# First batch entry's attention products in two sets of PSUM banks, the first inner blocks in accumulator banks, the first pair's scores head by head, and decoding order 1.5 places ahead

## The chip, the cores and the metric

One core of a Trainium2 chip runs the whole program. The metric is the device time in microseconds; times are medians over several executions. A measurement of this kernel tells 0.2% from no change.

## The reference

Windowed attention (8 batch entries, 8 heads, 576 positions, head size 64) and then a gated MLP over all 4608 tokens:

```python
def _attn_ref(q, k, v):
    window, dilation = 32, 4
    scores = scale * np.matmul(q, k.transpose(0, 1, 3, 2))
    rel = pos[:, None] - pos[None, :]
    mask_plain = (rel >= 0) & (rel < window)
    mask_dil = (rel >= 0) & (rel < window * dilation) & (rel % dilation == 0)
    ...  # first four heads plain, last four dilated
    scores = np.where(masks[None, :, :, :], scores, -1000000000.0)
    ...  # softmax over the keys
    return np.matmul(attn, v)

def _moe_ref(x, w_in, w_out):          # x: 4608 x 512, w_in: 512 x 2048, w_out: 2048 x 512
    h = x @ w_in
    g = h * (1.0 / (1.0 + np.exp(-1.702 * h)))
    return g @ w_out
```

q, k and v are float32, the two weights float64.

## The kernel before

**Work in order.** Heads go in pairs, so a batch entry has four pairs (k = 0 to 3 for the first). For each pair the scores are made (`scores`), the softmax runs on VectorE, ScalarE and GpSimd (`softmax`), the probabilities are transposed by VectorE (`ct`), and the product with v (`first_product` for the first entry) leaves the attention output in PSUM. It is drained as a high part (`xh`, by ScalarE) and a low part (`xl`, the remainder, by VectorE) in the tile `xs`; the last 64 positions go into `rests_x` and are stored for later. Then groups of 512 tokens run through the MLP. The first group, `main[0]`, starts as soon as the first entry's output is there; its inner blocks `up(f)` make 128 of the 2048 inner channels by twelve products of 128x512 (`hp_m`: three for each of four chunks of the model dimension), a gate (tanh on ScalarE, a multiply on VectorE), another split into `gh` and `gl`, and twelve products of the second matrix into four accumulator banks (`acc_m`). Attention of later entries runs between those products. After three such groups the rest runs in blocks of a seven-product scheme (`up_p`, `second_p` and so on), which the change does not touch.

**Decoding.** A weight arrives as float64 and is turned into two fp32r parts by `decode(n)`: two ScalarE steps, a sign step on ScalarE or VectorE, a shift on VectorE, an add on VectorE or GpSimd, a copy and a subtract. `order` says which weight comes as the n-th; each is 512 KB.

**PSUM.** There are eight banks: two under the tag `sp` (scores), one each under `hp` and `av`, and four which are first one tile `first_x` (pool `four`) and later the accumulators `acc0` to `acc3` (pool `quarters`, in the same place). All four products of the first entry write to `first_x`, each to one half of the columns of all four banks; the plan holds the four banks as one thing (`FOUR`), so a product waits until the one before it is drained. `hp_m_0` lies in `hp`, `hp_m_1` in `sp`, `hp_m_2` in `av`.

**What sets the order.** Every step is entered in a `Plan` with a cost per engine, an urgency, and the names that it reads and writes. The planner places all steps in time by these costs and writes the instructions of each engine in that order; in three further rounds (`ROUNDS`) it uses due times from the round before for all that lies behind `SINCE`. A step with a choice of engines goes where it ends first. While the plan shows PE idle in the first 60 us, it puts idle products in: small ones (32x16) early on, and 512-column products of `ident`, both into a tile in the bank `av`, by the function `warm`. An engine takes its instructions strictly in the written order. DMAs are issued on SP's queue (`load`).

Names that the prediction uses: L309 to L342 are the constants and masks; `plain` is the mask, brought into PSUM by a product with `ident` ahead of the scores; L490 the scores, L510 the maximum, L514 the exponential, L576 the first entry's products, L695 the transposes, L346, L348 and L353 the helpers `copy` and `pair`, L402, L403, L396 and L406 steps of `decode`, L863 the inner products, L872 the gate's multiply, L1258 and L1262 the idle products.

## Time and profile before

| | |
|---|---|
| median of three runs | 823.12 us (821.65 to 823.53) |
| profiled execution | 822.45 us, span 820.7 us |
| PE busy | 809.3 us, 99% of the span |
| VectorE, ScalarE, GpSimd busy | 669.0, 518.0, 328.4 us |
| chain that ended last | PE 97% |
| first inner product (L863) | at 25.62 us |
| mean granted clock of PE | 0.997 |

The span is cut by the profile into rows of instructions with a start, a duration and, in brackets, how long the engine stood idle before them and who ended that. "PE" is the matmul itself and "PEld" the weight load that stands with each; "issue" is time in which an engine waited for nothing that the profile shows.

### The profile page before, as it was taken

The page shows a single profiled execution, that of the slowest core. Times are in us where ns is not written, and L with a number is a line of the kernel's source. Part 1 is how long each engine was busy: PE and PEld are TensorE (multiplying, and loading weights), DVE is VectorE, ACT ScalarE, POOL GpSimd, SP SyncE. Part 2 cuts the span into 40 slices and gives each one's busy share as a digit, 9 for nine tenths or more (in the row PEclk, how much of TensorE's full clock was granted, in tenths as well). Part 3 has the DMA queues.
Part 4 walks back from the last instruction along what each step waited for, and adds up shares of the span by engine and source line. Part 5 has one row for each costly group of instructions (what it writes and reads, how often), then busy time and mean ns, then how long its engine had stood idle before and what let it go on. Part 6 is the DMA issues. An engine that isn't in the chain of part 4 may idle for free.

```text
span 820.7 us, 18890 instructions
## 1 busy us (share of the span) xinstructions
PE 809.3 (99%) x7279; PEld 653.4 (80%) x7279; DVE 669.0 (82%) x1081; ACT 518.0 (63%) x988; POOL 328.4 (40%) x294
## 2 busy tenths in 40 slices
PE   7999999999999999999999999999999999999997
PEld 4677878888887888778888888888888888888886
DVE  6898988888888876899889899996679885867575
ACT  7898986767577766786866654545456534544340
POOL 3442325455556553244345445531215332112251
PEclk9999999999999999999999999999999999999999
DMA  9577658899758657797788777775565658674545
GB/s 354 186 249 212 175 161 296 287 318 303 241 176 271 223 180 243 252 307 234 235 236 264 253 254 249 234 256 183 179 207 189 198 189 275 201 226 157 180 153 181
DMA packets 109610, 188.13 MB, mean 229 GB/s; under 512 B 26448, under 2 KB 55376, under 8 KB 109520
## 3 DMA queue, kind: packets, MB, share of 16 engines
q1 hardware_dynamic: 109376, 186.78, 70.2%
q8 instruction: 58, 0.95, 0.5%
q14 instruction: 32, 0.26, 0.1%
q10 hardware_dynamic: 144, 0.13, 0.0%
HBM read 140.64 MB, written 45.09 MB: 226 GB/s over the span
## 4 chain that ended last, share of the span: by engine, by line
PE 97%; DMA 1%; DVE 1%; issue 0%; ACT 0%; SPq 0%; DVEq 0%
PE hp_m L863 16%; PE up_p L1006 10%; PE up_r L1006 9%; PE up_q L1006 9%; PE acc_m L800 5%; PE second_p_Q L1121 5%; PE second_q_Q L1121 5%; PE acc_m L804 5%; PE acc_m L801 5%; PE second_r_Q L1121 5%; PE sp L490 4%; PE second_q_Z L1121 3%; PE second_r_Z L1121 3%; PE second_R L1121 3%; PE second_p_Z L1121 3%; PE av L608 2%
## 5 line engine op out<-in xcount | busy, mean ns | idle before, releaser
L353 POOL TENSOR_TENSOR arena<-arena 128x256 f32<-128x256 f32 (+3 forms) x94 | 100.7, 1083 | 97.8 <-DVE wi_last_units L353 21.6
L863 PE MATMUL hp_m<-xs,wi_kept 128*128 128x512 f32 x504 | 127.7, 396 | 1.2 <-DVE arena L872 0.9
L863 PEld LDWEIGHTS hp_m<-xs,wi_kept 128*128 128x128 f32 x504 | 92.9, 188 | 22.8 <-DVE arena L872 1.9
L353 POOL TENSOR_TENSOR wo_kept<-arena,wo_kept 128x512 fp32r<-128x512 f32 x41 | 56.9, 1395 | 131.5 <-ACT wo_kept L346 84.9
L346 ACT ACTIVATE wo_kept<-arena 128x512 fp32r<-128x512 f32 x111 | 69.2, 630 | 40.7 <-PE second_r_Q L1121 10.9
L1006 PE MATMUL up_r<-wi_kept,xs 128*128 128x512 f32 x336 | 85.3, 389 | 0.0
L1006 PE MATMUL up_p<-wi_kept,xs 128*128 128x512 f32 x336 | 84.2, 394 | 0.2 <-DVE arena L353 0.2
L1006 PE MATMUL up_q<-wi_kept,xs 128*128 128x512 f32 x336 | 83.4, 389 | 0.0
L1006 PEld LDWEIGHTS up_p<-wi_kept,xs 128*128 128x128 f32 x336 | 62.1, 188 | 14.7 <-DVE arena L353 0.9
L1006 PEld LDWEIGHTS up_q<-wi_kept,xs 128*128 128x128 f32 x336 | 63.0, 188 | 13.3 <-DVE arena L1028 0.3
L1006 PEld LDWEIGHTS up_r<-wi_kept,xs 128*128 128x128 f32 x336 | 63.1, 188 | 13.1
L353 DVE TENSOR_TENSOR wo_kept<-arena,wo_kept 128x512 fp32r<-128x512 f32 x80 | 61.1, 775 | 5.1 <-ACT wo_kept L346 4.7
L346 ACT ACTIVATE bt<-ct 32x256 f32<-32x256 f32 (+1 forms) x130 | 56.6, 435 | 11.7 <-DVE ct L534 6.0
L353 POOL TENSOR_TENSOR pr<-pr,sm 128x320 f32<-128x320 f32 x52 | 43.7, 856 | 48.5 <-DVE sm L518 43.5
L800 PE MATMUL acc_m<-gh,wo_kept 128*128 128x512 f32 x156 | 61.5, 394 | 0.0
L353 POOL TENSOR_TENSOR wo_kept<-wi_last_units,wo_kept 128x512 fp32r<-128x512 f32 x22 | 29.9, 1361 | 78.3 <-ACT wo_kept L346 72.3
L353 DVE TENSOR_TENSOR arena<-arena 128x512 f32<-128x512 f32 (+1 forms) x75 | 59.1, 797 | 2.7 <-ACT arena L346 1.8
L801 PE MATMUL acc_m<-gh,wo_kept 128*128 128x512 f32 x156 | 60.8, 390 | 0.0
L1027 ACT ACTIVATE arena<-arena 128x512 f32<-128x512 f32 x60 | 37.4, 628 | 33.4 <-DVE arena L353 27.2
L1028 DVE SCALAR_TENSOR_TENSOR arena<-arena 128x512 f32<-128x512 f32 x60 | 49.8, 837 | 1.7 <-ACT arena L1027 1.3
L346 ACT ACTIVATE gh<-arena 128x512 fp32r<-128x512 f32 x57 | 36.0, 631 | 17.5 <-DVE arena L872 5.8
L353 DVE TENSOR_TENSOR gl<-arena,gh 128x512 fp32r<-128x512 f32 x53 | 41.3, 779 | 6.5 <-ACT gh L346 3.2
(267 smaller groups left out, 1824.7 us busy)
## 6 DMA issues: line engine op xcount, KB each, us to landing
xs<-sums SPq DMA_DIRECT2D x168, 256.0 KB, 3.3
out_weights<-sums_o SPq DMA_DIRECT2D x63, 512.0 KB, 3.5
qk<-qk_dram SPq DMA_DIRECT2D x29, 576.0 KB, 4.4
xs<-sums_o SPq DMA_DIRECT2D x21, 512.0 KB, 3.8
v<-vp_dram SPq DMA_DIRECT2D x28, 320.0 KB, 4.1
sums_o<-arena SPq DMA_DIRECT2D x32, 256.0 KB, 3.2
sums<-arena SPq DMA_DIRECT2D x32, 256.0 KB, 2.9
arena<-wi_dram SPq DMA_DIRECT2D x15, 512.0 KB, 4.7
```

The lines of the kernel that those rows point to most:

```text
L346: A.activation(dst, src, AF.Copy, scale=scale)
L353: (V if e == DVE else G).tensor_tensor(out=dst, in0=a, in1=b, op=op)
L490: T.matmul(dst[:, w:w + n], u["qk"][rows, at:at + 32], u["qk"][rows, S + first:S + first + n], start=not masked(k), stop=True, tile_positi ...
L608: T.matmul(u["x"][i][rows, at:at + last - first], u["v"][keys, a, m], bt[keys, m, a, first:last], start=(bank_, a) not in begun, stop=True ...
L800: T.matmul(self.acc[j], w[:, 0, cols], high, start=f == 0, stop=False)
L801: T.matmul(self.acc[j], w[:, 1, cols], high, start=False, stop=False)
L804: T.matmul(self.acc[j], w[:, 0, P * j:P * j + P], low, start=False, stop=f == NF - 1)
L863: T.matmul(hps[f], wi(f)[:, st, cols], mv[:, c], start=c == 0 and k == 0, stop=c == NC - 1 and k == 2)
L1006: T.matmul(self.banks[place], xs[:, slot, at:at + P], wi_kept[:, 2 * a + c, mv], start=fresh and c == 0 and k == 0, stop=c == 1 and k == 2 ...
L1027: add({ACT: 0.60}, -10.0, lambda e: A.activation(unit(tmp), src(), AF.Tanh, scale=0.851), need, own(tmp))
L1028: add({DVE: -0.70 if need[0][0] == "A" else 0.70}, -10.0, lambda e: V.scalar_tensor_tensor(out=unit(dst), in0=unit(tmp), scalar=1.0, in1=s ...
L1121: T.matmul(self.second[key], w[:, st, cols], mv, start=fresh and y == 0 and k == 0, stop=y == 1 and k == 2, skip_group_check=True)
```

## The change

- The first entry's products alternate between two sets of four banks: pairs 0 and 2 in `first_x`, pairs 1 and 3 in the two banks of `sp` and in `hp` and `av`. Each pair of a set has its own columns. A product then no longer waits for the drain of the product before it, and the drains of pairs 1 and 3 come in three pieces, one for each tile.
- The first two inner blocks of the first group go to the accumulators `acc2` and `acc3`, since `sp`, `hp` and `av` are held by pairs 1 and 3; the third stays in `av`.
- Pair 0's q and k come in two transfers, one for each head, and its scores are two steps, one for each head.
- The decoding order is sorted by f for the first matrix and f + 1.5 for the second: wi0, wi1, wo0, wi2, wo1, wi3, wo2, wi4, where it was wi0, wi1, wo0, wi2, wo1, wo2, wi3, wo3.
- Pair 0's v is loaded later (urgency -4.5 instead of -6.7), `SINCE` is 140 instead of 130, and `warm` now gives no idle products from the moment at which pair 1's banks are taken.

```diff
-ROUNDS, SINCE, CALM, ROOM = 3, 130.0, 8.0, 3.0
+ROUNDS, SINCE, CALM, ROOM = 3, 140.0, 8.0, 3.0
-    order = [(0, 0), (0, 1), (1, 0), (0, 2)]
-    order += [(i % 2, i // 2) for i in range(2 * NF) if (i % 2, i // 2) not in order]
+    order = sorted(((out_, f) for f in range(NF) for out_ in range(2)), key=lambda b: b[1] + 1.5 * b[0])
...
-    FOUR = tuple(f"acc{j}" for j in range(NC))
+    SETS = tuple(f"acc{j}" for j in range(NC)), ("sp", "hp", "av")
...
+        if k == 0:
+            for a in range(2):
+                add({DMA: 295}, -9.0, lambda e, a=a: work(e, slice(D * a, D * a + D)), (), (("qk0", "head1")[a],))
+            return
...
-        u["x"] = first_x[:, :, ROW * (k % 2):ROW * (k % 2) + ROW]
+        cols = slice(ROW * (k // 2), ROW * (k // 2) + ROW)
+        if k % 2:
+            if "others" not in misc:
+                misc["others"] = bank([P, 2, GT], "sp", "first_sp"), *(bank([P, GT], n, f"first_{n}") for n in ("hp", "av"))
+            sp, hp, av = misc["others"]
+            u["x"] = [sp[:, :, cols], hp[:, None, cols], av[:, None, cols]]
+            parts = [sp[:, 0, cols], sp[:, 1, cols], hp[:, cols], av[:, cols]]
+        else:
+            u["x"] = [first_x[:, :, cols]]
+            parts = [first_x[:, g, cols] for g in range(4)]
...
-        add({PE: 1.5 if k else 2.3}, k - 1.0e5, lambda e: scores(k), (lots(k)[0],), ("sp", f"scores{k}"), count=180)
+        if k == 0:
+            for a in range(2):
+                add({PE: 0.75}, k - 1.0e5, lambda e, a=a: scores(k, (a,)), (("qk0", "head1")[a],), ("sp", f"scores{k}"), count=90)
+        else:
+            add({PE: 1.5}, k - 1.0e5, lambda e: scores(k), (lots(k)[0],), ("sp", f"scores{k}"), count=180)
...
-            FOUR, count=184)
+            SETS[k % 2], count=184)
...
-            place = {1: "sp", 2: "av"}.get(f, "hp") if self is main[0] else "hp"
+            place = {0: "acc2", 1: "acc3", 2: "av"}.get(f, "hp") if self is main[0] else "hp"
...
     def warm(i):
-        if 2 not in main[0].hps:
+        if "others" not in misc:
```

The written order shows the change on PE at two places. First the head of PE's program, before (idle products into `idle`, then the masks and scores of pair 0, `sp`; a number in a name only tells tiles apart):

```order
L1262 MATMUL idle<-ones 32x16 x49
L478 LDWEIGHTS ident
L478 MATMUL sp_189<-plain,ident 128x320
L478 LDWEIGHTS ident
L478 MATMUL sp_189<-plain,ident 128x320
L490 MATMUL sp_189<-qk_128 32x64 x35
```

The same place in the changed kernel, where L485 is the mask and L497 the scores:

```order
L1291 MATMUL idle<-ones 32x16 x44
L485 LDWEIGHTS ident
L485 MATMUL sp_183<-plain,ident 128x320
L497 MATMUL sp_183<-qk_128 32x64 x19
L497 MATMUL sp_183<-qk_128 32x48
L497 MATMUL sp_183<-qk_128 32x16
L485 LDWEIGHTS ident
L485 MATMUL sp_183<-plain,ident 128x320
```

There are five small idle products fewer, and the second head's mask has moved behind the first head's scores.

Second, PE before from pair 2's product on (`ct` is the transposed probabilities, v of pairs 1 to 3 lies in `arena`, `hp_m_0` and `hp_m_1` are the first two inner blocks); idle products stand between these rows and the products around them:

```order
L576 MATMUL first_x<-ct_91,arena 64x64 x24
L576 MATMUL first_x<-ct_91,arena 64x48 x8
L576 MATMUL first_x<-ct_91,arena 64x16 x8
L863 MATMUL hp_m_0_578<-xs,wi_kept 128x512 x3
L863 MATMUL hp_m_1_585<-xs,wi_kept 128x512 x3
```

In the changed kernel pair 3's product ends, and the inner blocks follow, as here:

```order
L592 MATMUL first_sp<-ct_92,arena 64x16 x4
L592 MATMUL first_hp<-ct_92,arena 64x16 x2
L592 MATMUL first_av<-ct_92,arena 64x16 x2
L892 MATMUL hp_m_0_668<-xs,wi_kept 128x512 x12
L892 MATMUL hp_m_1_695<-xs,wi_kept 128x512 x12
L892 MATMUL hp_m_2_718<-xs,wi_kept 128x512 x6
```

The inner products no longer come by threes between the attention products: all four of these stand first, with no idle products between them, and then whole inner blocks. (Idle products stand between the four sets of scores in both; those numbers are 2, 6 and 10 before, and 4, 10 and 11 now.)

Third, ScalarE in the changed kernel from pair 1's drain to pair 2's (`xs` are the high parts, `arena<-first_av` pair 1's rest, the L395 row is the 16-bit sign step of a decode):

```order
L346 ACTIVATE xs<-first_sp 128x288
L346 ACTIVATE xs<-first_hp 128x144
L346 ACTIVATE xs<-first_av 128x80
L346 ACTIVATE arena<-first_av 128x64
L346 ACTIVATE wo_kept<-arena 128x512
L395 ACTIVATE arena<-arena 128x512
L346 ACTIVATE xs<-first_x 128x4x128
```

Pair 1's high part has come apart into three pieces, and pair 2's stands behind a weight split and a sign step. On VectorE pair 2's low part stands as follows:

```order
L724 STREAM_TRANSPOSE ct_92<-pr_84 128x320 x2
L348 COPY arena<-first_x 128x4x16
L353 ISA arena<-bt,arena 128x1024
L353 TENSOR_TENSOR xs<-first_x,xs 128x4x128
```

Behind pair 3's transposes come pair 2's rest, one decode step, and then pair 2's low part.

## The prediction

> **What bounds the kernel now.** I read the page first: its busy line, and the chain that ended last.

> ```profile
> span 820.7 us, 18890 instructions
> PE 809.3 (99%) x7279; PEld 653.4 (80%) x7279; DVE 669.0 (82%) x1081; ACT 518.0 (63%) x988; POOL 328.4 (40%) x294
> PE 97%; DMA 1%; DVE 1%; issue 0%; ACT 0%; SPq 0%; DVEq 0%
> q8 instruction: 58, 0.95, 0.5%
> ```

> TensorE is 99% busy and carries 97% of the chain. The change does not touch the number of 512-column products, so it can move the time in three ways only: the moment from which PE has unbroken work, PE's clock around that moment, and the few stops after it. The timeline of PE gives the first (columns: start, us, then the group; a row's us run past the start of the next, because matmuls overlap).

> ```profile
> 1.02 1.56 PE L1262 MATMUL idle<-ones 32*32 32x16 f32 x98 [1.02 <-DVE ones L309]
> 4.27 0.69 PE L478 MATMUL sp<-plain,ident 128*128 128x320 bf16 x2 [1.69 <-DVE plain L332]
> 4.89 1.45 PE L490 MATMUL sp<-qk 64*32 64x64 f32 x84
> 6.27 0.72 PE L1262 MATMUL idle<-ones 32*32 32x16 f32 x38
> 6.92 1.16 PE L1258 MATMUL idle<-ident 128*128 128x512 bf16 x2
> ...
> 9.38 1.45 PE L490 MATMUL sp<-arena 64*32 64x64 f32 x84
> 10.76 2.74 PE L1258 MATMUL idle<-ident 128*128 128x512 bf16 x6
> ...
> 13.97 1.13 PE L490 MATMUL sp<-arena 64*32 64x64 f32 x84
> 15.03 2.33 PE L1258 MATMUL idle<-ident 128*128 128x512 bf16 x10
> 17.20 0.43 PE L478 MATMUL sp<-arena,ident 128*128 128x320 bf16 x2
> 17.56 0.86 PE L490 MATMUL sp<-arena 64*32 64x64 f32 x65
> 20.25 0.37 PE L490 MATMUL sp<-arena 64*32 64x64 f32 x19 [1.83 <-issue]
> 20.55 1.49 PE L576 MATMUL first_x<-ct,v 32*64 32x32 f32 x92
> 21.96 2.63 PE L1258 MATMUL idle<-ident 128*128 128x512 bf16 x6
> 24.53 1.16 PE L576 MATMUL first_x<-ct,arena 32*64 32x32 f32 x92
> ...
> 31.68 1.08 PE L576 MATMUL first_x<-ct,arena 32*64 32x64 f32 x80
> 32.69 7.11 PE L863 MATMUL hp_m<-xs,wi_kept 128*128 128x512 f32 x27
> ```

> The four sets of scores (L490) and the four attention products (L576) are spread over the first 33 us with idle products between them. From 32.69 PE runs without a hole to speak of. Twelve hp matmuls are already done by then (two groups of six behind the second and third product), and twelve take 2.72 us by the chain's row below. So the unbroken work is worth a start at 32.69 - 2.72 = 29.97 us. That is the number the change has to beat.

> ```profile
> 58.35 2.72 PE hp_m L863 x12
> 33.00:45.00 12.00, 11.82 (x80) 8.90 (x81) 10.78 (x19) 11.15 (x19) 3.88 (x3) 1.00 0.74 261
> 100.00:130.00 30.00, 29.05 (x407) 22.70 (x406) 25.61 (x46) 24.73 (x52) 8.69 (x10) 1.00 0.59 170
> PE hp_m L863 <- DVE arena L872: 0.9, 1, 0.9
> ```

> The two rows of windows (busy time of PE first) show nearly all that PE still loses before the tail: 0.18 us before 45, and 0.95 in one wait for VectorE's gate (L872) between 100 and 130.

> **Two things at the start that the change meets.** One is the stop of 1.83 us at 18.4, inside the scores of pair 3, put down to "issue". Count the rows up to it: idle 98+38+18, masks 8 (two per set), scores 3x84+65, together 479 matmuls, each with a weight load: 958 instructions. The page has 58 instruction transfers for 2x7279 PE instructions, 251 each, so I take blocks of 256, and the stop lies at an edge, 192+3x256 = 960. The transfers of single stretches (5.0 to 6.1, and 17.7 to 18.9; the stretch 22.0 to 23.2 reads as the second) hold one each:

> ```profile
> q8 instruction: 1, 0.02, 5.3%
> q8 instruction: 1, 0.02, 5.8%
> ```

> PE passed the edge before (704) in the scores of pair 2, 34 rows in, at 13.97 + 34/84 x 1.06 = 14.4; the block came between 17.7 and 18.9 and was usable at 20.25, so 1.35 us after it landed and 5.85 us after that passing. After the edge at 20.25 the next block came by 23.2 and was usable at about 24.5: 4.25 us. I call these the lead times. [...]

> The other is the clock. I cut the start into stretches of 3.41 us along the change of the granted clock (PE busy, granted clock, DMA share, GB/s):

> ```profile
> 7.29:10.71 3.42, 2.77 (x88) 1.00 1.01 402
> 17.53:20.95 3.42, 1.59 (x124) 1.00 1.03 403
> 20.95:24.36 3.41, 3.41 (x78) 0.50 0.80 282
> 24.36:27.77 3.41, 3.41 (x133) 1.00 0.43 109
> ```

> The stretch with the stop has PE busy 1.59 of 3.42, and the next one runs at half clock. It shows in the idle products: 0.43 us each from 21.96, against 0.217 from 15.03. The ones from 10.76 take 0.42 as well although their clock is printed as 1.00 (no record had come yet), so a stretch with 2.77 busy, mostly small tiles, did not lift the clock either. Half clock costs small tiles less: 1.41 against 1.09 us for a 92-row product.

> **The change, part by part.**

> Scores of pair 0, head by head. The PE work is the same; the wait for the whole of q and k (0.4 before 4.89) goes, since the mask's own wait ends at 4.27 and a half transfer lands before. VectorE now takes the maximum at once (it had a decode step in front) and pair 1's q and k travel ahead of pair 0's v, 0.4 MB or 1.0 us of a bus at 402 GB/s. So the scores of pair 1 could start at about 8.4 instead of 9.38. One more issue on SP (under half a microsecond) is hidden, since the bus, not SP, is the bound there; pair 0's v comes some 5 us later and is still there long before 20.

> But the early idle products are 44 instead of 49: 176 instructions instead of 196, so PE no longer passes the first edge (192) at about 2.4 us in idle work. It passes it in head 0 of the scores, at about 4.6. With the lead times seen (4.9 for the first block of before: passed at 2.5, landed by 6.1, plus 1.35; and 5.85) the next block is usable between 9.5 and 10.5; I take 10.0, for the bus is as full there as at 14. The scores of pair 1 reach that edge 44 rows in, at 8.4 + 0.7 = 9.1, wait 0.9 and end at 10.7. Before: 10.76. That gain is gone.

> From there on: ten idle products (8 at 0.43, the rest at 0.22) to 14.5; mask 0.36 and scores of pair 2, 1.06, to 15.9; edge 704 passed at about 15.8, so the next block is usable at 21.65. Eleven idle products to 18.3, mask, scores of pair 3 (0.95; no edge in them now) to 19.7. Product 0 follows at once, meets edge 960 after 23 of 92 rows and stops at 20.0 until 21.65. It ends at 22.7 (69/92 of 1.41), against 21.96. Product 1 has its own banks and needs no wait, but meets edge 1216 at 23.6, stops until 21.65 + 4.25 = 25.9 and ends at 26.4. In before it ended at 25.62. The second bank set thus saves product 1 a wait that ends no earlier.

> Then the drains, with their rows (ScalarE first, then VectorE):

> ```profile
> 22.09 0.66 ACT L346 ACTIVATE xs<-first_x 128x432 fp32r<-128x432 f32 x2 [1.07 <-PE first_x L576]
> 23.93 0.63 ACT L346 ACTIVATE wo_kept<-arena 128x512 fp32r<-128x512 f32 x1
> 28.11 1.37 ACT L396 ACTIVATE arena<-arena 128x512 f16<-128x512 f32 x1
> 29.20 1.20 ACT L346 ACTIVATE xs<-first_x 128x512 fp32r<-128x512 f32 x1
> ...
> 27.22 0.90 DVE L695 STREAM_TRANSPOSE ct<-pr 128x320 f32<-128x320 f32 x2
> 28.89 0.28 DVE L348 COPY arena<-first_x 128x64 f32<-128x64 f32 x1 [0.77 <-PE first_x L576]
> 30.44 1.14 DVE L353 TENSOR_TENSOR xs<-first_x,xs 128x512 fp32r<-128x512 f32 x1 [0.92 <-ACT xs L346]
> 36.28 0.68 DVE L353 CUSTOM_DVE_ANT_0 arena<-arena 128x1024 uint16<-128x1024 uint16 x1
> ```

> Product 2 runs behind product 1 (26.4 to 27.5). On ScalarE, in its new order, stand pair 1's high parts in three pieces (0.8, against two pieces in 0.66), its rest (0.1), a weight split (0.54 from start to start) and a 16-bit step (1.09): 26.4 + 0.8 + 0.1 + 0.54 + 1.09 = 28.9. Then pair 2's high part, 1.2, to 30.1. On VectorE pair 2's rest (0.15), a decode step (0.6) and pair 2's low part (1.14) follow: 32.0. Product 3 waits for the transposes (0.90) behind pair 1's low parts, runs from about 28.8, and is done by 30.3: not the last. The first block's output now lies in a bank of the first set (acc2), which pair 2 must leave first, and that is why it starts at 32.0, not after the first chunk. All twelve of its matmuls are then still to come: 32.0 against 29.97, **+2.0**. Ends of this term: 29.4, if blocks come in time (third case), and 33, if the first two lead times stretch by another half microsecond each.

> Clock. The idle products stop for good once product 1 has taken the bank "av": the function that emits them returns nothing then. Between 20.95 and 32.0 PE has only small tiles and its waits: of 3.41 us stretches 2.1 busy (rest of product 0, part of product 1), then 1.6, then 1.5, the measure of the stretch that went before a half clock (1.59). So I expect half clock when the first block starts. With boundaries where they are, the next is at 24.36 + 3x3.41 = 34.6: 2.6 us at half rate cost **+1.3**. Bounds: 0 if the clock is full, 2.6 if the boundary falls so that five microseconds pass. [...]

> The stops after 33. PE starts its blocks 2 to 3 us later against the same decode, and wi1 to wi3 come a place earlier, so the 0.18 and the 0.95 have cover: **-1.1** (ends -1.1 and, since the whole later order is rewritten by SINCE = 140, +1.5 for one new wait of the size of that 0.95 and its refill). Decoding order, the later v, the 14 more and 2 fewer small VectorE and ScalarE instructions behind 32 us I cost at nothing: VectorE was busy 10.78 of 12 us between 33 and 45 and PE lost only 0.18.

> Sum: 2.0 + 1.3 - 1.1 = +2.2 us. The profiled execution took 822.45 (span 820.7 and 1.75 around it); it would be 824.65. It lies 0.67 under the median of the three timed runs, 823.12, so the forecast is 825.2 as a median.

> **Cases.** A measurement of this kernel tells 0.2% (1.65 us) from no change.

> 1. As summed, 0.68: 825.2, own range 823.6 to 827.0. For it: every edge lies where the rows put it. About two thirds of this case are over 1.65.
> 2. The clock stays full, 0.14: +0.9, 824.0, no difference. [...]
> 3. Faster, 0.09: instruction blocks come within about 4 us of the passing, so that products 0 and 1 do not stop. The two stops, 1.65 and 2.3 us, hold product 1's end back by 3.9; without them the steps of ScalarE and VectorE between the drains set the pace, and I let two thirds of the 3.9 through: the first block at 29.4. With a full clock that is 29.4 - 29.97 - 1.1 = -1.7, 821.4; it decides only if both hold, otherwise it is no difference.
> 4. A new wait later, 0.09: the sum and 1.5 more, 826.7.

> Slower: two thirds of 0.68 and nearly all of the fourth, 0.54; same 0.38; faster 0.08. The range 822.8 to 827.2 leaves out the third case's best end and the worst of the fourth.

> **What the profile after would show.** Right: an issue stop in the first or second product, a half clock in the stretch in which L892 starts, its first matmuls 0.43 us apart, first L892 at 31 to 33 us, and no wait for VectorE near 109. Wrong: products 0 and 1 without a stop and L892 before 30, or L892 at 0.23 from its first matmul. A wait for decoded weights in the first three blocks would break the third term.

## The result and the profile after

The changed kernel takes 831.33 us (median of four executions, 830.22 to 833.59) against 823.04 (821.65 to 823.53) for the kernel before: ratio 1.0107, 95% interval 1.0081 to 1.0133. It is slower by 8.3 us, where +2.2 was forecast. The profiled execution took 830.22 us, its span is 828.4, so 7.7 us more span than before.

The page of the changed kernel, its span, its busy times and the chain that ended last:

```profile
span 828.4 us, 18794 instructions
PE 809.9 (98%) x7225; PEld 654.8 (79%) x7225; DVE 671.9 (81%) x1094; ACT 512.9 (62%) x988; POOL 322.5 (39%) x289
PE 87%; DVE 5%; DMA 2%; issue 1%; ACT 1%; POOL 0%; DVEq 0%; ACTq 0%; POOLq 0%
```

PE is busy for about as long as before (809.9 against 809.3 us). Nearly all of the loss is time in which PE stands, or runs at half clock. The timeline of PE shows where, with the same columns as before:

```profile
1.02 1.37 PE L1291 MATMUL idle<-ones 32*32 32x16 f32 x88 [1.02 <-DVE ones L309]
...
4.86 1.32 PE L497 MATMUL sp<-qk 64*32 64x64 f32 x42 [0.17 <-DMA qk<-qk_dram]
6.12 0.45 PE L485 MATMUL sp<-plain,ident 128*128 128x320 bf16 x1
6.49 1.32 PE L497 MATMUL sp<-qk 64*32 64x64 f32 x42
...
10.26 1.20 PE L497 MATMUL sp<-arena 64*32 64x64 f32 x84
11.39 2.33 PE L1287 MATMUL idle<-ident 128*128 128x512 bf16 x10
14.24 0.43 PE L485 MATMUL sp<-arena,ident 128*128 128x320 bf16 x2 [0.52 <-DVE sm L525]
14.60 0.99 PE L497 MATMUL sp<-arena 64*32 64x64 f32 x75
17.31 0.42 PE L497 MATMUL sp<-arena 64*32 64x64 f32 x9 [1.72 <-issue]
17.67 4.09 PE L1287 MATMUL idle<-ident 128*128 128x512 bf16 x11
21.59 0.43 PE L485 MATMUL sp<-arena,ident 128*128 128x320 bf16 x2
21.96 1.07 PE L497 MATMUL sp<-arena 64*32 64x64 f32 x84
22.96 1.54 PE L592 MATMUL first_x<-ct,v 32*64 32x32 f32 x92
...
27.37 0.27 PE L592 MATMUL first_av<-ct,arena 32*64 32x64 f32 x2 [1.69 <-issue]
31.11 0.77 PE L592 MATMUL first_sp<-ct,arena 32*64 32x64 f32 x5 [1.89 <-DVE ct L724]
34.73 5.62 PE L892 MATMUL hp_m<-xs,wi_kept 128*128 128x512 f32 x17 [1.77 <-DVE xs L353]
```

Three places differ from what was forecast. Each head of pair 0 takes 1.26 us by itself (4.86 to 6.12), where both together took 1.38 before (4.89 to 6.27). The stop at edge 704 is now in the scores of pair 2 (17.31, 1.72 us). And eleven idle products run at half clock from 17.67 to 21.59, ahead of the scores of pair 3. The first inner product starts at 34.73, 4.8 us behind the 29.97 that the work of before was worth.

The windows (PE busy first, then PEld, VectorE, ScalarE, GpSimd, the granted clock, the DMA share and GB/s), first along the change of the clock, then the later stretch that was shown of before:

```profile
14.00:17.41 3.41, 1.45 (x84) 1.12 (x85) 2.99 (x8) 3.41 (x7) 3.02 (x4) 1.00 1.02 404
17.41:20.82 3.41, 3.41 (x17) 1.38 (x18) 2.95 (x5) 2.56 (x5) 1.67 (x3) 0.50 1.02 407
24.24:27.65 3.41, 1.36 (x114) 1.17 (x100) 3.19 (x9) 2.80 (x6) 1.33 (x2) 1.00 0.05 18
27.65:31.06 3.41, 1.57 (x110) 1.46 (x93) 3.41 (x8) 2.60 (x7) 2.00 (x3) 0.50 0.51 156
34.48:37.89 3.41, 3.16 (x8) 2.51 (x9) 3.29 (x9) 2.30 (x6) 0.07 (x1) 0.50 0.18 41
100.00:130.00 30.00, 29.84 (x276) 23.55 (x274) 25.86 (x47) 26.60 (x53) 11.65 (x9) 1.00 0.56 170
```

The clock is halved twice, each time behind a stretch with 1.4 us of PE work. The second time it stays so until 37.89, so the first 3.16 us of inner products run at half rate and lose about 1.6.

How much PE stands behind 45 us is read from one window over 745 us, before and after:

```profile
45.00:790.00 745.00, 743.70 (x6249) 605.68 (x6227) 614.96 (x980) 473.96 (x920) 301.09 (x262) 1.00 0.71 229
45.00:790.00 745.00, 742.26 (x6240) 603.59 (x6240) 614.28 (x985) 470.94 (x918) 296.76 (x259) 1.00 0.71 229
```

PE is idle for 745 - 743.70 = 1.30 us before and 2.74 after. Start 4.8, clock 1.6 and these 1.4 more make 7.8, against 7.7 us measured. This splits the loss of one execution; another one of the same first 130 us splits it differently (see after_since130). The largest waits of PE behind the start are now three for VectorE's gate (L901), 1.1 us in all; the 0.95 near 109 is gone:

```profile
PE hp_m L892 <- DVE arena L901: 1.1, 3, 0.5
```

Last, the transfers. The windows from 3.30 to 5.50 of before and of after, and the first decode step on ScalarE, which waits for wi0, of before and of after:

```profile
3.30:5.50 2.20, 1.23 (x46) 0.71 (x50) 0.53 (x6) 1.19 (x3) 0.21 (x1) 1.00 0.97 373
3.30:5.50 2.20, 1.06 (x25) 0.64 (x28) 0.53 (x6) 1.19 (x3) 0.22 (x1) 1.00 1.04 237
5.96 0.66 ACT L402 ACTIVATE arena<-arena 128x512 f32<-128x512 f32 x1 [0.68 <-DMA arena<-wi_dram]
8.55 0.67 ACT L401 ACTIVATE arena<-arena 128x512 f32<-128x512 f32 x1 [3.26 <-DMA arena<-wi_dram]
```

While the halves of q and k travel, the bus moves 237 instead of 373 GB/s at about the same busy share (1.04 against 0.97), and wi0, next in the queue, is there 2.6 us later.

### The profile page after: what moved, and what is told of

It reads as the page before. It is cut to its first block, busy times and chain, and to the rows that moved or that the text cites. A ratio compares the mean times of both kernels' runs of the same rounds, so it can differ in the third digit from the quotient of the medians.

```text
span 828.4 us, 18794 instructions
## 1 busy us (share of the span) xinstructions
PE 809.9 (98%) x7225; PEld 654.8 (79%) x7225; DVE 671.9 (81%) x1094; ACT 512.9 (62%) x988; POOL 322.5 (39%) x289
## 4 chain that ended last, share of the span: by engine, by line
PE 87%; DVE 5%; DMA 2%; issue 1%; ACT 1%; POOL 0%; DVEq 0%; ACTq 0%; POOLq 0%
PE hp_m L892 14%; PE up_q L1035 9%; PE up_r L1035 9%; PE up_p L1035 8%; PE second_q_Q L1150 5%; PE second_r_Q L1150 5%; PE second_p_Q L1150 5%; PE acc_m L829 4%; PE acc_m L833 4%; PE acc_m L830 4%; PE sp L497 3%; PE second_r_Z L1150 3%; PE second_q_Z L1150 3%; PE second_p_Z L1150 3%; PE second_R L1150 3%; PE av L624 2%
## 5 line engine op out<-in xcount | busy, mean ns | idle before, releaser
L353 POOL TENSOR_TENSOR arena<-arena 128x256 f32<-128x256 f32 (+3 forms) x101 | 108.8, 1085 | 145.0 <-DVE arena L353 23.6
L892 PE MATMUL hp_m<-xs,wi_kept 128*128 128x512 f32 x504 | 128.6, 398 | 2.9 <-DVE xs L353 1.8
L892 PEld LDWEIGHTS hp_m<-xs,wi_kept 128*128 128x128 f32 x504 | 94.1, 190 | 24.7 <-DVE arena L901 2.0
L346 ACT ACTIVATE wo_kept<-arena 128x512 fp32r<-128x512 f32 x117 | 73.0, 630 | 40.0 <-PE second_r_Q L1150 9.4
L353 POOL TENSOR_TENSOR wo_kept<-arena,wo_kept 128x512 fp32r<-128x512 f32 x34 | 46.6, 1376 | 100.2 <-ACT wo_kept L346 95.3
L353 POOL TENSOR_TENSOR wo_kept<-wi_last_units,wo_kept 128x512 fp32r<-128x512 f32 x28 | 38.5, 1376 | 116.4 <-ACT wo_kept L346 101.2
L353 DVE TENSOR_TENSOR wo_kept<-arena,wo_kept 128x512 fp32r<-128x512 f32 x87 | 60.6, 708 | 6.2 <-ACT wo_kept L346 5.7
L353 POOL TENSOR_TENSOR pr<-pr,sm 128x320 f32<-128x320 f32 x52 | 44.0, 858 | 45.4 <-DVE sm L525 42.0
L346 ACT ACTIVATE bt<-ct 32x256 f32<-32x256 f32 (+1 forms) x122 | 53.1, 436 | 10.5 <-DVE ct L541 7.3
L353 DVE TENSOR_TENSOR arena<-arena 128x512 f32<-128x512 f32 (+1 forms) x74 | 56.3, 767 | 0.4
L353 DVE TENSOR_TENSOR gl<-arena,gh 128x512 fp32r<-128x512 f32 x54 | 42.2, 782 | 9.8 <-PE acc_m L833 4.9
L346 ACT ACTIVATE gh<-arena 128x512 fp32r<-128x512 f32 x57 | 36.2, 635 | 22.2 <-DVE arena L901 7.7
```

Of the source, the lines that this page charges most:

```text
L346: A.activation(dst, src, AF.Copy, scale=scale)
L353: (V if e == DVE else G).tensor_tensor(out=dst, in0=a, in1=b, op=op)
L892: T.matmul(hps[f], wi(f)[:, st, cols], mv[:, c], start=c == 0 and k == 0, stop=c == NC - 1 and k == 2)
```

## The experiments

The kernels are compared by two numbers of the trace beside the time. "Start" is what the unbroken work is worth: the start of the first inner product behind the last attention product, less 0.227 us (2.72/12) for each inner product done before. "Idle" is 745 us less PE's busy time between 45 and 790. The time is the median, the ratio goes against the kernel before on the same chip. Start and idle are of the one profiled execution, whose time stands beside them; it lies up to 2.5 us from the median.

| kernel | time, us | ratio (95%) | profiled, us | start | idle |
|---|---|---|---|---|---|
| before | 823.0 to 823.5 | 1 | 822.45 | 30.0 | 1.3 |
| changed kernel | 831.33 | 1.0107 (1.0081-1.0133) | 830.22 | 34.7 | 2.7 |
| before_heads | 831.42 | 1.0098 (1.0081-1.0114) | 831.69 | 33.9 | 5.0 |
| before_sets | 830.88 | 1.0094 (1.0075-1.0114) | 830.54 | 32.2 | 4.3 |
| before_v45 | 830.48 | 1.0095 (1.0080-1.0110) | 832.67 | 33.3 | 5.5 |
| before_order | 826.78 | 1.0037 (1.0027-1.0047) | 825.67 | 30.4 | 3.6 |
| before_since | 826.85 | 1.0040 (1.0025-1.0054) | 828.72 | 31.9 | 4.1 |
| whole | 827.59 | 1.0052 (1.0036-1.0069) | 827.51 | 31.6 | 4.4 |
| oneload_head_scores | 829.79 | 1.0075 (1.0058-1.0092) | 830.01 | 33.0 | 4.0 |
| halves_whole_scores | 829.95 | 1.0078 (1.0063-1.0093) | 830.27 | 33.5 | 4.2 |
| after_one_set | 828.47 | 1.0065 (1.0042-1.0088) | 828.57 | 33.1 | 3.3 |
| after_since130 | 834.28 | 1.0130 (1.0110-1.0150) | 834.46 | 33.7 | 5.0 |
| after_fewer_idle | 829.21 | 1.0072 (1.0045-1.0098) | 831.71 | 33.7 | 3.4 |
| after_more10 | 829.25 | 1.0074 (1.0056-1.0091) | 830.68 | 33.9 | 3.7 |
| after_more46 | 831.46 | 1.0103 (1.0081-1.0125) | 831.36 | 35.2 | 3.8 |
| before_less24 | 827.47 | 1.0045 (1.0029-1.0060) | 827.69 | 33.2 | 1.8 |
| before_less24b | 825.40 | 1.0026 (1.0013-1.0038) | 825.82 | 31.4 | 2.4 |
| before_delay | 826.89 | 1.0039 (1.0026-1.0051) | 827.30 | 33.8 | 1.7 |
| whole_idle | 828.82 | 1.0061 (1.0046-1.0076) | 828.64 | 33.2 | 4.8 |
| whole_idle2 | 827.47 | 1.0046 (1.0028-1.0064) | 827.55 | 32.0 | 4.2 |

A start is that of one execution and moves by itself: before_since has the program of before up to 130 us, and its start came out 1.9 us later; after_since130 has that of the changed kernel, and its start came out 1.1 earlier. So starts are trusted to about 1 to 2 us, and medians decide. For the changed kernel start, clock and idle add up to the measured loss; for the others the same sum comes out between 1.6 us too high and 2.8 too low, so it shows where time goes, and not to the last microsecond.

The theories are named by letters. S: the split of pair 0 sets the start back. B: the bank sets do. L and O: the later order costs; O says that every newly made order behind has stops of its own. D: the later stops come from the late start. E: it is the places of the edges of instruction blocks. C: one stretch of 3.4 us without a hole lifts the clock.

### The parts alone, on the kernel before

Pair 0's split (with the later v), the bank sets, the decoding order and SINCE, each put into the kernel before by itself.

```diff
 before_heads:
+            for a in range(2):
+                add({DMA: 295}, -9.0, lambda e, a=a: work(e, slice(D * a, D * a + D)), (), (("qk0", "head1")[a],))
 before_sets:
+    SETS = tuple(f"acc{j}" for j in range(NC)), ("sp", "hp", "av")
+            place = {0: "acc2", 1: "acc3", 2: "av"}.get(f, "hp") if self is main[0] else "hp"
 before_order:
+    order = sorted(((out_, f) for f in range(NF) for out_ in range(2)), key=lambda b: b[1] + 1.5 * b[0])
 before_since:
+ROUNDS, SINCE, CALM, ROOM = 3, 140.0, 8.0, 3.0
 before_v45:
+        add({DMA: 390 if k < NC else 328}, (-4.5, -6.7, -3.8, -1.6)[k] if k < NC else 1.6 * k - 0.3, work, waits(k),
```

before_heads:

> The kernel before with only the split of pair 0 (two transfers, two steps of scores, v later). Theory S: wi0 lands near 8.5, scores 0 end near 7.7, scores 3 end 2 us later than before (near 22.5 instead of 20.5), and the time is 3 us or more over before, 826 to 828. Theory B: within 1 us of before, 822 to 824.

before_sets:

> The kernel before with only the two sets of banks, the first inner blocks in accumulators, and the idle products that end with pair 1's product. Theory S: within 1.5 us of before, 822 to 824.5, the first inner product (all chunks ready) at 30 to 31.5. Theory B: 825 to 829, with half clock over the first inner block and stops for instructions in products 0 and 1.

Both came out above the higher end, at 831.4 and 830.9. Each alone costs nearly as much as all parts together, so S and B are both too simple. The trace of before_heads has the start 3.9 us later, as S says (scores 3 end at 22.6), but idle time rises by 3.7 as well. In before_sets the start is 2.2 later, the half clock lasts from about 22.2 to 35.9, and idle time rises by 3.0.

before_order:

> The kernel before with the new decoding order alone. By the prediction's third term the wait for the gate near 109 loses its cause and the time falls by up to 1.1 us, 822.3 to 823. By theory O new stops come in its place, 824 to 827, with the start within 0.5 us of before. By theory D within 0.8 us of before.

before_since:

> The kernel before with SINCE = 140 alone: nothing of the first 130 us changes, the written order behind is made anew. Theory O (each new order behind 130 us brings its own stops of PE, of which the kernel before happens to have few: 1.1 us listed in it, 2.2 to 5.7 in the five kernels whose start was changed): the first inner block starts as before, stops add up to 2.5 to 5 us, and the time is 824.5 to 827.5. Theory D (the later stops come from the later or faster start): 822.7 to 824.

Both land where theory O puts them, at +3.3 us each. SINCE alone changes no instruction of the first 130 us, and the median still rises by 3.3, with 2.8 us more of idle time behind 45 in the profiled execution (828.72 us, a slower one than the median of 826.85). Two of the new stops of before_since, the first for a gate that VectorE makes late:

```profile
226.91 1.66 PE L863 MATMUL hp_m<-xs,wi_last 128*128 128x512 f32 x6 [0.91 <-DVE arena L872]
373.44 0.97 PE L1121 MATMUL second_p_Q<-wo_kept,out_weights 128*128 128x512 f32 x3 [0.94 <-DMA out_weights<-sums_o]
```

before_v45:

> The kernel before with pair 0's v alone loaded later (-4.5 instead of -6.7), so that pair 1's q and k travel ahead of it. If the 1 us of the bus brings the scores of pair 1 forward and nothing else changes: the first inner block 0 to 1 us earlier, 822 to 823.5. By theory O, since the plan is made anew: stops of 2 to 5 us behind 33 us, 824 to 827.

It costs 7.3 us (830.48), more than either forecast. The scores of pair 1 did not come sooner (they start at 10.16, against 9.38), and product 1 now waits 2.40 us. On ScalarE pair 0's high part stands behind a decode step (L396), at 25.65 instead of 22.09, and VectorE's low part follows it until 27.3:

```profile
25.65 0.72 ACT L346 ACTIVATE xs<-first_x 128x432 fp32r<-128x432 f32 x2
27.39 1.55 PE L576 MATMUL first_x<-ct,arena 32*64 32x32 f32 x92 [2.40 <-ACT wo_kept L346]
```

Its idle time is the highest of all, 5.5, in an execution 2.2 us above its median. A part that I had costed at nothing costs 7.3 us alone, and nearly as much as together with the split (before_heads contains it, 8.0). So before_heads doesn't tell what the split alone costs; the three kernels of the next part come nearer. Split with later v, sets, decoding order and SINCE add up to 8.0 + 7.4 + 3.3 + 3.3, some 22 us; together they make 8.3. They don't add. Each makes the planner write a new order, which by itself can cost what SINCE costs.

### Parts undone in the changed kernel

```diff
 whole (both), oneload_head_scores (the first only), halves_whole_scores (the second only):
-            for a in range(2):
-                add({DMA: 295}, -9.0, lambda e, a=a: work(e, slice(D * a, D * a + D)), (), (("qk0", "head1")[a],))
+            add({DMA: 590}, -9.0, work, (), ("qk0", "head1"))
...
-            for a in range(2):
-                add({PE: 0.75}, k - 1.0e5, lambda e, a=a: scores(k, (a,)), (("qk0", "head1")[a],), ("sp", f"scores{k}"), count=90)
+            add({PE: 1.5}, k - 1.0e5, lambda e: scores(k), ("qk0", "head1"), ("sp", f"scores{k}"), count=180)
 after_one_set (and the lines of the two sets in drains and products likewise):
-    SETS = tuple(f"acc{j}" for j in range(NC)), ("sp", "hp", "av")
+    FOUR = tuple(f"acc{j}" for j in range(NC))
-            place = {0: "acc2", 1: "acc3", 2: "av"}.get(f, "hp") if self is main[0] else "hp"
+            place = {1: "sp", 2: "av"}.get(f, "hp") if self is main[0] else "hp"
 after_since130:
-ROUNDS, SINCE, CALM, ROOM = 3, 140.0, 8.0, 3.0
+ROUNDS, SINCE, CALM, ROOM = 3, 130.0, 8.0, 3.0
```

whole:

> The changed kernel, with pair 0's q and k in one transfer again and its scores in one step (bank sets, decoding order, later v and SINCE stay). Theory S (the split of pair 0 sets the start back: its two transfers of 64 partitions run at half the rate, and the heads' scores no longer overlap): wi0 lands near 6 us instead of 8.5, scores 0 end near 6.3 instead of 7.7, the first inner product starts at 31.5 to 32.5 instead of 34.7, and the time is 827.5 to 829 against 831.3. Theory B (the bank sets, with the stops for instructions between the products, set it back): the start stays at 34 or later, 830 to 832. Theory L (the later order costs): start earlier or not, the time stays within 1 us of 831.

oneload_head_scores:

> The changed kernel with one transfer for pair 0's q and k, but its scores still head by head in two steps. If of theory S the bus is what costs: wi0 lands near 6, and the time comes within 0.5 us of the kernel with both undone. If the heads' order on PE is what costs: scores 0 take 2.6 us instead of 1.4, and the time is 1 us or more above the kernel with both undone. Theory B: no difference from the changed kernel in either, 830 to 832.

halves_whole_scores:

> The changed kernel with pair 0's q and k in two transfers of 64 partitions, but its scores in one step; its idle products are those of the kernel with pair 0 whole (827.6), so no edge moves against that one. If the half transfers cost by the bus: wi0 lands near 8.5 instead of 6, the first inner block 1 us or more later than 31.6, and the time is 828.6 to 829.6. If they cost nothing and the rest of the split's price is edges: 827.2 to 828.2.

whole took 827.59, as S says: without the split 3.7 of the 8.3 us are gone. That isn't the price of the split alone, since the later order is written anew too, and idle time rises from 2.7 to 4.4.

The two halves of the split are priced more cleanly. In whole, oneload_head_scores and halves_whole_scores VectorE and ScalarE carry out the same instructions in the same order over the whole span (but for a few that lie up to three places apart), so the later order is the same, and idle time is alike (4.4, 4.0, 4.2). With one transfer and scores head by head the time is 2.2 us more than whole, with half transfers and whole scores 2.4 more; no execution of either was as fast as the slowest of whole (828.74 and 829.31 at the least, against 828.58). The scores of pair 1 start at 9.28 to 9.52 in the three profiles with the head of whole (whole, whole_idle, whole_idle2), and at 10.96 and 10.87 in these two.

The two forms of the scores, and wi0's arrival on ScalarE, in whole, in oneload_head_scores and in halves_whole_scores:

```profile
5.25 1.45 PE L495 MATMUL sp<-qk 64*32 64x64 f32 x84 [0.29 <-DMA qk<-qk_dram]
6.49 0.68 ACT L401 ACTIVATE arena<-arena 128x512 f32<-128x512 f32 x1 [1.20 <-DMA arena<-wi_dram]
```

```profile
5.36 1.32 PE L495 MATMUL sp<-qk 64*32 64x64 f32 x42 [0.67 <-DMA qk<-qk_dram]
6.99 1.31 PE L495 MATMUL sp<-qk 64*32 64x64 f32 x42
6.58 0.66 ACT L401 ACTIVATE arena<-arena 128x512 f32<-128x512 f32 x1 [1.29 <-DMA arena<-wi_dram]
```

```profile
8.32 0.66 ACT L401 ACTIVATE arena<-arena 128x512 f32<-128x512 f32 x1 [3.03 <-DMA arena<-wi_dram]
```

So half transfers alone hold wi0 back (8.32 against 6.49 and 6.58), and the heads' order alone lengthens the scores (8.23 - 5.36 = 2.9 us with the second mask, against 1.4). The rate was read in the changed kernel: from 3.30 to 5.50 the bus moved 237 GB/s where it moved 373 before, from 3.50 to 5.50 216 where it moved 366, and 415 from 7.18 to 10.59, when the halves were through. The half rate of theory S is thus 0.52 to 0.64 in these windows. Why a transfer to 64 partitions moves less was not shown.

after_one_set:

> The changed kernel without the two sets of banks (all products in the four banks of before, the first inner blocks in hp, sp and av, idle products as before); split of pair 0, later v, decoding order and SINCE as in the changed kernel. If the sets cost what they cost alone (7.4 us over before): 824 to 826. If the start is set by the split, whichever banks are used (the kernel with the split alone has its unbroken work worth a start at 33.9, the changed kernel at 34.7): 829.5 to 832.

It took 828.47, between the two: in the changed kernel the sets cost about 2.9 us, less than alone (the intervals of the two ratios just overlap), and the start is only 1.6 us earlier without them. Its mean granted clock was 0.998, against 0.991 in the changed kernel, so part of the 2.9 is likely the half clock over the first inner block.

after_since130:

> The changed kernel with SINCE = 130 again: the first 130 us are the same. If each written order behind has stops of its own, whatever the start (theory O): the first inner block at 34 to 35 as in the changed kernel, the stops behind it differ from its 2.2 us by 1 us or more, mostly for the worse (seen so far: 1.1 to 5.7), 830 to 834. If the order behind doesn't matter here: 830.8 to 831.8.

834.28 is 3 us above the changed kernel by the medians, with the same first 130 us, as theory O says; but the ratios (1.0130, interval 1.0110 to 1.0150, against 1.0107, 1.0081 to 1.0133) overlap, so this is likely and not certain. What came in the profiled execution is a group of waits on PE, the longest for steps on ScalarE, and behind it PE runs at half clock from 352.8 to 359.6:

```profile
351.17 0.97 PE L497 MATMUL sp<-qk 64*32 64x64 f32 x72 [1.26 <-ACT arena L346]
355.00:360.00 5.00, 4.31 (x11) 2.94 (x11) 3.80 (x7) 2.07 (x4) 0.00 (x0) 0.54 1.00 375
```

SINCE = 140 is thus 3 us worse for the kernel before and, as it seems, some 3 us better for the changed kernel. Nothing here gives it a worth of its own.

This run is also a second execution of the changed kernel's start, and it shows which part of the first was chance. The stop in scores 2 is there (1.36 us), but the clock is not halved behind it:

```profile
17.41:20.82 3.41, 3.41 (x99) 1.97 (x97) 3.05 (x5) 2.94 (x5) 1.43 (x3) 1.00 1.05 413
```

The eleven idle products take 2.4 us there, and the scores of pair 3 start at 19.80, not 21.96. Product 0 then stops at edge 960 for 1.72 us, the clock is halved from 25.11 to 38.76, and the first inner product starts at 33.65.

### The edges of instruction blocks

These keep the written order and only add idle products or leave some out, so nothing behind is planned anew.

```diff
 before_less24 (before_less24b: if 49 < n <= 61):
+            if n <= 12:
+                return
             col = 32 * (n % 4)
 after_more10 (after_more46: 24 instead of 6):
+            for _ in range(6 if n == 1 else 1):
 after_fewer_idle:
+                n = misc["big"] = misc.get("big", 0) + 1
+                if 16 < n <= 25:
+                    return
                 T.matmul(misc["idle"], ident, ident[:, None, :].broadcast_to([P, GT // P, P]), start=True, stop=True)
```

before_less24:

> The kernel before without 12 of the small idle products at its head (24 matmuls, 48 instructions), the written order otherwise the same. If the stop in the scores of pair 3 hangs on the count of instructions (edges at 192 + 256 j): the edge moves 24 matmuls on, scores 3 run through (84 in one row, ended near 18.7 instead of 20.6), and the stop lies in the first rows of product 0, until 20 to 21.5; the time is within 0.8 us of before, since product 0 still ends near 22. If it hangs on something else (the bus, a moment): it stays at the 66th matmul of scores 3.

before_less24b:

> The kernel before without 24 small idle matmuls again, but those behind the scores of pair 0 instead of those at the head; PE passes the first edge in idle work at 2.5 us as before. If the 4.3 us of the other place came from the late passing of the first edge (theory E): no stops in the scores of pairs 1 and 2, scores 3 run through and end near 18.7, the stop lies 5 matmuls into product 0 until 20.5 to 21, product 0 ends near 21.8 as before (21.96), and the time is 822.3 to 823.8, no difference or a little less. If 24 matmuls fewer cost by shifting the later edges: 825 or more, as there.

The count is right to the matmul: the stop moved from the 66th matmul of scores 3 to the 6th of product 0, 24 matmuls on. But before_less24 also stops at four places that I had not expected (the scores of pairs 1 and 2, products 1 and 2), and costs 4.3 us by the medians for 24 matmuls less. Rows of before_less24 with their stops:

```profile
11.65 1.18 PE L490 MATMUL sp<-arena 64*32 64x64 f32 x63 [1.19 <-issue]
17.93 0.45 PE L490 MATMUL sp<-arena 64*32 64x64 f32 x27 [1.19 <-issue]
20.84 1.07 PE L490 MATMUL sp<-arena 64*32 64x64 f32 x84
24.12 1.11 PE L576 MATMUL first_x<-ct,v 32*64 32x32 f32 x87 [1.98 <-issue]
```

The three stops lie 128 matmuls apart (63 + 6 + 2 + 57 and 27 + 10 + 2 + 84 + 5 in the rows of PE), with their weight loads 256 instructions. PE passes the first edge (192) in the scores of pair 0 there, at about 5.5 us, and then stops at each edge in turn: first 6.2 us or so apart (usable again at 11.65, 17.93 and 24.12), then 3.8 apart (0.42 us until 27.93 and 0.34 until 31.71). In before_less24b, with the first edge passed early again, the first of these stops is gone:

```profile
15.85 0.44 PE L490 MATMUL sp<-arena 64*32 64x64 f32 x27 [1.43 <-issue]
22.05 1.30 PE L576 MATMUL first_x<-ct,v 32*64 32x32 f32 x87 [1.98 <-issue]
```

Its time is 2.3 us over before, not the 0 that I gave it. So by the medians about half of the 4.3 comes from the late first edge and half from the places of the later ones, though the two intervals (1.0029 to 1.0060 and 1.0013 to 1.0038) overlap. Both ways of moving its edges made the kernel before slower, and small idle products at its head, which look like nothing, are part of where they lie.

after_more10:

> The changed kernel with the five small idle products back that its head has fewer than before (10 matmuls, 20 instructions; they fit in the wait for the mask). PE passes the edge at 192 instructions in idle work at about 2.4 us again, not in the scores, and all later edges lie 10 matmuls earlier. If the missed early edge sets the instruction blocks back (theory E): the stop in the scores of pair 2 shrinks or goes, the first inner block starts 1 to 2 us earlier, 829 to 830.5. If the half transfers and the heads' order alone set the start: the stop of 1.7 us stays, 10 matmuls earlier, and the time is 830.8 to 832.

after_more46:

> The changed kernel with 23 more small idle products at its head (46 matmuls, 92 instructions, 0.7 us, within the wait for the mask). All edges lie 46 matmuls earlier: the second in the idle products behind scores 0, the third at the 30th matmul of scores 2, the next in scores 3 and in product 1. Theory E: no stop in scores 2, the clock is not halved at 17.4, scores 3 start near 19.5 to 20, the first inner block at 32 to 33.5, 828 to 830. If the transfers and the heads' order alone set the start: 830.8 to 832.

after_fewer_idle:

> The changed kernel with 2 instead of 11 idle products between the scores of pairs 2 and 3; the written order is otherwise the same. If these products hold scores 3 back (they ran to 21.6 at half clock, while its bank was free at 19.5): scores 3 start near 19.5, the first inner block 1 to 2 us earlier (32.7 to 33.7), and the time is 829.3 to 830.3 against 831.3. If instruction blocks or the drains behind set the start: scores 3 earlier, but products 0 and 1 stop the longer, the first inner block at 34.3 or later, 830.8 to 832.

Ten matmuls back at the head gave 829.25, within what theory E says, but the interval touches that of the changed kernel, and the stop in scores 2 stayed (0.72 us in this execution; 1.36 in after_since130, whose head is that of the changed kernel). So 2 us are possible, not shown.

after_more46 missed: no stop in scores 2, but the next in scores 3 (1.64 us), the mask 0.5 later behind the longer idle work, and 831.46.

after_fewer_idle came out as the first theory says: scores 3 start at 19.51 instead of 21.96, the first inner block at 33.74, and the median is 829.21; product 0 then stops for 1.29 us. But its trace can't prove it: the profiled execution took 831.71, as long as the changed kernel, and after_since130, with all eleven idle products, started its scores 3 and its inner block just as early. What PE waits for is the block: in the seven kernels with pair 0 split in both ways (the changed kernel, the five named after_, and before_heads) edge 960 is passed between 22.86 and 23.51, whatever stands in front of it, where the kernel before passes it at 20.25. Each edge that is moved away from one place stops PE at another, where PE has less time between two of them than the next block takes (5.6 to 6.8 us in the first 24 us).

### A late start by itself, and the clock

```diff
 before_delay, behind pair 3's product (whole_idle2: ten, into the bank av):
+                for n in range(40):
+                    T.matmul(first_x[:, n % NC, 2 * ROW:2 * ROW + 192], ident, ident[:, None, 0:64].broadcast_to([P, 3, 64]),
+                             start=True, stop=True, skip_group_check=True)
 whole_idle, in warm:
+        if "others" in misc and misc.setdefault("more", 5) and i is not None:
+            misc["more"] -= 1
+            for g in (0, 2):
+                T.matmul(first_x[:, g, 2 * ROW:2 * ROW + 192], ident, ident[:, None, 0:64].broadcast_to([P, 3, 64]), start=True,
+                         stop=True, skip_group_check=True)
```

before_delay:

> The kernel before, its written order unchanged, with 40 more idle products of 192 columns behind pair 3's product, unknown to the planner: PE's unbroken work starts later by 40 x 192/512 x 0.217 = 3.3 us, and nothing else moves. By the prediction's third term the wait of 0.95 near 109 vanishes, and the time is 2.2 to 2.6 us over before (825.5 to 826). If a late start costs its whole length: 3.3 over (826.6). If a late start brings stops of its own (theory D): 4.5 us or more over (827.8 or more).

826.89: its ratio of 1.0039 is 3.2 us (interval 2.1 to 4.2), which fits a late start that costs its whole length, and excludes the 4.5 of theory D. The interval alone would leave room for the 2.2 to 2.6 of my third term; the trace decides that. The wait near 109 is still there, 4.3 us later and as long as before:

```profile
113.58 1.66 PE L870 MATMUL hp_m<-xs,wi_kept 128*128 128x512 f32 x6 [0.94 <-DVE arena L879]
```

Theory D falls, and so does my term of cover. The engines behind PE are late together with it. The four kernels that keep the order of before have 1.3 to 2.4 us of idle time, with starts from 30.0 to 33.8; the sixteen with another order have 2.7 to 5.5. Idle time goes with the order: the four kernels with the order of the changed kernel have 2.7 to 3.8, and the five with the order of whole 4.0 to 4.8.

whole_idle:

> The changed kernel with pair 0 whole, and ten more idle products of 192 columns (1.6 us at half clock) in the gap of 1.5 us between pair 3's product and the first inner block. Theory C (a stretch of 3.4 us without a hole is what lifts the clock): the granted clock is full one stretch earlier, at about 32.2 instead of 35.6, the first inner products 0.23 us apart from there, and the time is 1 to 1.7 us less than without them (825.9 to 826.6 against 827.6). If the holes of 1.7 and 2.4 us further up hold the clock down, or the gap was covered anyway: no difference, 827.3 to 828.

whole_idle2:

> The changed kernel with pair 0 whole, and ten idle products of 192 columns straight behind pair 3's product, in its own bank av, where nothing is to be waited for (in the kernel with idle products in first_x they waited for VectorE's drain and came after the gap). Theory C (one stretch of 3.4 us without a hole lifts the clock): the gap of 1.5 us is filled, the granted clock is full a stretch earlier where the stretch's boundaries allow it, and the time is up to 1.7 us less than without them, 826 to 827.3 against 827.6. If the clock doesn't hang on that gap: 827.3 to 828.3.

The first did not do what it should: its idle products waited 1.56 us for a VectorE drain of the bank that they write to, and then lay in front of the inner block (828.82, 1.2 us more by the medians). The second filled the gap, from 30.39 to 32.01, and gained nothing (827.47 against 827.59). Two of its stretches say why:

```profile
27.95:31.36 3.41, 2.81 (x115) 2.71 (x116) 1.28 (x5) 3.22 (x5) 1.75 (x3) 0.50 0.53 172
31.36:34.77 3.41, 3.41 (x13) 2.62 (x11) 3.41 (x8) 2.67 (x7) 0.89 (x1) 0.51 0.20 43
```

The stretch with 2.81 us of work did not lift the clock, the next, full one did, at 34.77. So it goes in all twenty traces. Cut each into stretches of 3.41 us at the recorded changes of its clock: up to 48 us the clock rose from half to full eighteen times, each time behind a stretch with at least 3.16 us of PE work, and never behind one with 2.83 or less. It fell eighteen times, sixteen of them behind a stretch with 1.01 to 1.85 us of work and twice behind 2.16; it stayed full behind no stretch with less than 1.79. Between 1.79 and 2.16 both happened, so the lower bound isn't sharp. A stop that a boundary cuts in two can thus leave the clock full, as the 2.67 us did in before_delay:

```profile
16.76:20.18 3.42, 1.87 (x71) 1.04 (x69) 2.56 (x6) 3.39 (x6) 2.18 (x4) 1.00 1.03 403
```

The next stretch there has 2.29 us of work. Where the boundaries fall differs from execution to execution: with the same first 130 us, the clock was halved at 17.41 and 27.65 in the changed kernel, and at 25.11 in after_since130.

## Why the prediction was wrong, point by point

The sign was right and the size was not: +2.2 forecast, +8.3 measured, outside the range. The sign is no proof of the account: two steps on pair 0 that were to cost nothing cost over 2 us each, the term of the later stops had the wrong sign, and parts that were put at nothing cost 3 us and more alone.

**"The PE work is the same" (scores head by head).** This step failed. The work per matmul is the same, but two heads on different halves of the rows had run beside each other: 84 matmuls in 1.38 us. One head alone takes 1.26 for 42. oneload_head_scores puts the price at 2.2 us over whole. The gain forecast for VectorE went with it: its maximum could start only behind the second head's scores, at 7.87.

**"A half transfer lands before 4.27", and the scores of pair 1 at 8.4.** Failed too. The first half itself came nearly in time (PE waited 0.17 us for it, until 4.86); what the step left out is that the bus slows down to 237 GB/s while the halves travel and that wi0 behind them comes 2.6 us later. halves_whole_scores: 2.4 us over whole. The scores of pair 1 started at 10.26, not at 8.4. Against the 9.38 of before that is later, but the same program of before started them at 10.14 in before_since. What both steps cost together in one and the same order was not measured; whole, with a new order, takes 3.7 us away.

**The edges.** The count of 256 and the places were right (the stops of before_less24 lie 256 instructions apart, and in before_less24b the stop of scores 3 moved on by the 24 matmuls that it leaves out), and so was the claim that five idle products fewer make PE pass the first edge late. What I had wrong is edge 448. PE came to it at 10.8, not at 9.1, and the block was there, no stop. The block of 704 then came 6.5 us behind that passing, not 5.85, so the stop came there instead, and with the clock halved at 17.4 the eleven idle products took 3.9 instead of 2.4 us. I had priced idle products as filling, not as work in the way. What that cost in the end is 0.6 us at most by these traces: in after_since130, where they ran at full clock, and in after_fewer_idle, where nine of them were gone, product 0 went on from edge 960 at 22.98 and 22.90, against 23.51.

**Start, +2.0.** It measured +4.8 in the profile, and +3.7 in after_since130, whose first 130 us are the same. Without the split it is +1.6 (whole), near the forecast; but the program of before itself gave 29.97 and 31.87, so how much of the term the bank sets are worth stays open. "Product 3 is not the last" held: the inner block waits for pair 2's low part (xs, L353) as forecast, but 2.7 us later than the 32.0. Product 1 stopped at edge 1216 as forecast, but until 27.4 instead of 25.9, and ended at 28.0 instead of 26.4. The other 1.1 us came between the drains, where the forecast has no wait at all:

```profile
29.93 0.63 ACT L346 ACTIVATE wo_kept<-arena 128x512 fp32r<-128x512 f32 x1 [0.81 <-DVE arena L353]
33.51 1.08 DVE L353 TENSOR_TENSOR xs<-first_x,xs 128x512 fp32r<-128x512 f32 x1
```

ScalarE was in a decode step until 28.2, and the weight split in its order waited 0.81 us for VectorE, with pair 2's high part behind it.

**Clock, +1.3.** It measured about +1.6, half clock until 37.89. This term held, in size and in its reason: a stretch with little PE work, here 1.36 us, came before the half clock. The second case, a full clock, didn't come: the clock was halved behind gaps of 1.72 and 1.69 us, shorter than the 1.83 of before. But a short gap doesn't always do it: before_delay had a stop of 2.67 us in scores 3, cut in two by a boundary, and its clock stayed at 1.00.

**Later stops, -1.1.** The sign was wrong: idle time behind 45 us rose by 1.4. The wait near 109 went, as forecast, but not for the reason given, since a late start leaves it in place (before_delay). It went with the new order, and not for the decoding order either: it is absent from before_heads, before_sets and before_v45 too, which decode in the old order. Such a new order brings 1.4 to 4.2 us more idle time than before has, in each of the sixteen traces (nine orders). My upper end of +1.5 "for one new wait" is passed by every one of them but the changed kernel itself (1.44).

**Parts costed at nothing.** The later v, the decoding order and SINCE cost 7.3, 3.3 and 3.3 us alone, each with the new order that it brings. What each costs inside the changed kernel is not known.

No kernel here beats the kernel before.

## What to carry to other kernels

Where a planner writes the order, price the re-planning itself: make the same kernel with a neutral change of its numbers (here SINCE alone, 3.3 us) and take that cost as the least width of the forecast, ahead of any mechanism. Do parts of a bundle alone, but don't add them up: here four alone make some 22 us and together 8.3. And before a step is split in two to start earlier, look at what its two halves share: two heads side by side on PE (2.2 us by oneload_head_scores) and one whole transfer (2.4 us by halves_whole_scores) were worth more than the earlier start. To price such a step, keep the written order the same, as the three kernels with the order of whole do.
